# Attention, soft-MoE routing and FFN on one core: the routing's steps placed by a table in place of a queue

## Chip, cores and metric

One core of a Trainium2 chip runs the whole program in one launch. The metric is the device time of an execution in microseconds, the median of several runs.

## What is computed

Three layers follow each other: masked attention with ALiBi-like biases (4 batches, 8 heads, 768 tokens, head size 64, each token sees its last 96 keys and 8 global ones), a soft mixture of experts (32 slots, 8 experts), and a feed-forward layer with a squared ReLU.

```python
scores = scale * np.matmul(q, k.transpose(0, 1, 3, 2)) + bias     # masked to local and global keys
a = np.exp(scores - scores.max(-1)); a = a / (a.sum(-1) + 1e-09)
x = (a @ v) as (3072, 512)
logits = x @ phi                                                  # (3072, 32)
d = softmax(logits, axis=0); slot_input = d.T @ x                 # over all tokens
slot_out[e] = np.maximum(slot_input[e] @ w1[e], 0.0) @ w2[e]
c = softmax(logits, axis=1); y = c @ slot_out
out = np.maximum(y @ w_in, 0.0) ** 2 @ w_out
```

## The kernel before

The attention is cut into 48 units: a batch, a pair of query tiles of 128 tokens, and a pair of heads. Four units make a chunk of 256 tokens with all heads; there are 12 chunks. One pass of the loop at line 548 (`for i in range(2, NU - 4, 2)`) handles two units, so a chunk takes two passes. What TensorE does in a pass is the same each time, in this order: `stage_T` (line 265) turns the two units' weights `sm` with 16 transposes of 128x128 into four PSUM tiles `pt`; `stage_qk` (225) makes the scores `s` of a unit four ahead; `stage_pv` (281) multiplies the copied `pT` by the values into `o`, for both units; a second `stage_qk` makes another `s`. In the first chunk of a batch's three, some tiles have one key tile in place of two, so 12 transposes and narrower scores. Around it VectorE masks the scores and finds their maxima (`stage_max`, line 237, eight instructions a pass) and copies the first `pt` tile of each unit to `pT`; ScalarE takes the exponentials (`stage_exp`, 256), copies the second `pt` tile of each unit, and copies `o` to `xT` (`stage_x`, 299).

PSUM has eight banks here: four take the scores (tag `s`), four everything else (tag `m`, `bank` in line 305): the four `pt` tiles of a pass, the two `o`, and what the routing needs.

The routing is the generator `route` (323). For each finished chunk k it makes the logits and adds the chunk to the running softmax over tokens. Its `yield`s cut it into steps. For an odd k (a "front") there are six: the logits' matmuls `lt` (16 rows in the profile, line 362), their copies by ScalarE and VectorE, four transposes `pl` (372), then VectorE's `rc`, `lh`, and the reduction into `c_tok` with the first four transposes `px` of the chunk's output (341), then VectorE's multiply of `px` into `xb` (344) and the other four `px`, and the last multiply. An even k ("back") goes on after that for two chunks at once: a transpose `pq` of `c_tok` (413), a maximum and two exponentials (428 to 433), a transpose `pd` (445), its copy `db` and `rden`, a matmul `pS` of 4 x 512 columns (470), and the update of `acc` (488): eleven steps.

Which step runs where is set by `queue` and `step` (493 to 501). A chunk's route is appended when the chunk is done (line 550); `step(n)` lets the oldest route in the queue go n steps on. A pass calls it after the scores (`step(1)`, 567), after the second exponentials (`step(1)`, 572) and at its end (`step(2)`, 590); in the first pass of a chunk also right behind the units' transposes (554). Each engine runs its instructions in the program's order, so a step that is called elsewhere stands elsewhere on TensorE, VectorE and ScalarE. Which bank a tile gets is chosen when the program is built, by which one comes free first in that order.

After the loop (`K, L = LAST, LAST + 1`) the last two chunks' routing is written out by hand, then come the experts' layers and the feed-forward layer, whose weights SP loads as buffers come free.

Of the kernel before, what the change touches and what calls it, by code (L numbers as in the profile page):

```python
# [21 lines left out]
NPR = H // 2  # L22
# [17 lines left out]
def attention_moe_ffn(ctx: ExitStack, tc, qk, vx, nn, phi, w1, w2, w_in, w_out, consts, relw, out):  # L40
# [60 lines left out]
    def load_qk(i):  # L101
        b, tp, pr = units[i]
        r = early.pop("raw", None) if i == 0 else raw_tile(i)
        n = 5 if tp == 0 else 6
        nc.sync.dma_start(r[:, 0:n], qk[b, tp, pr][:, 0:n])
        raws[i] = r

    def load_v(i):
        b, tp, pr = units[i]
        v = early.pop("v", None) if i == 0 else v_tile(i)  # L110
        n = 3 if tp == 0 else 4
        nc.sync.dma_start(v[:, 0:n], vx[b, tp, pr][:, 0:n])
        vals[i] = v
# [58 lines left out]
    def make_flag():  # L172
        V.tensor_scalar(fl[:, 0:1], n_f[0:1, 0:1], 1.0, None, op0=ALU.is_lt)
        V.scalar_tensor_tensor(fl[:, 0:1], n_f[0:1, 0:1], float(LMAX), fl[:, 0:1], op0=ALU.is_gt, op1=ALU.add)
        V.scalar_tensor_tensor(fl[:, 0:1], n_f[0:1, 1:2], 0.0, fl[:, 0:1], op0=ALU.not_equal, op1=ALU.add)
        V.scalar_tensor_tensor(fl[:, 0:1], n_f[0:1, 2:3], 0.0, fl[:, 0:1], op0=ALU.is_lt, op1=ALU.add)
        V.scalar_tensor_tensor(fl[:, 0:1], n_f[0:1, 2:3], float(GMAX), fl[:, 0:1], op0=ALU.is_gt, op1=ALU.add)
        V.scalar_tensor_tensor(fl[:, 0:1], n_f[0:1, 3:4], 0.0, fl[:, 0:1], op0=ALU.not_equal, op1=ALU.add)
        V.tensor_copy(gen_i, fl[:, 0:1])
# [19 lines left out]
    def load_w(i, part=0, parts=1):  # L199
        name, src, shape, dt = items[i]  # L200
        if name == first[0][0]:

            t = slot(SLOTS[i], [P, 2, shape[1]], dt, "raw_0")
            for j in range(2):
                wt[first[j][0]] = t[:, j, :]
        elif SLOTS[i] == "s0":
            wt[name] = [slot(f"s0{h}", [P, 4, DM], dt, f"{name}{h}") for h in "ab"]
            for h in range(2):
                nc.sync.dma_start(wt[name][h], src[:, 4 * h : 4 * h + 4])
            return  # L210
        elif part == 0 and name != first[1][0]:
            wt[name] = slot(SLOTS[i], shape, dt, name)
        n = shape[1] // parts
        ps = slice(part * n, part * n + n)
        nc.sync.dma_start(wt[name][:, ps], src[:, ps])
# [9 lines left out]
    def stage_qk(i):  # L225
        b, tp, pr = units[i]
        r = raws.pop(i)
        sc = [aps.tile([P, 2, 2, P], F32, tag="s", name=f"s{i}_{hh}", bufs=4) for hh in range(2)]
        for tt in range(2):
            n = width(tp, tt)  # L230
            for hh in range(2):
                r0 = hh * D
                rhs = r[r0 : r0 + D, 2 + tt : 3 + tt, :] if n == 1 else r[r0 : r0 + D, 2 + tt : 6 - tt : 3 - 2 * tt, :]
                nc.tensor.matmul(sc[hh][:, tt, 0:n, :], lhsT=r[r0 : r0 + D, tt, :], rhs=rhs, start=True, stop=True)  # L234
        st[i] = [sc]

    def stage_max(i, tt):
        b, tp, pr = units[i]
        if tt == 0:
            st[i].append(att.tile([P, 4, 2, P], F32, tag="sm", name=f"sm{i}", bufs=3))  # L240
            st[i].append(att.tile([P, 4], F32, tag="nm", name=f"nm{i}", bufs=3))
        sc, sm, nm = st[i]
        n = width(tp, tt)
        for hh in range(2):
            j = 2 * tt + hh
            m = masks[2 * pr + hh]
            V.tensor_tensor_reduce(  # L247
                out=sm[:, j, 0:n, :], in0=sc[hh][:, tt, 0:n, :], in1=m[:, 2:3, :] if n == 1 else m[:, 0:2, :], scale=-QK_SCALE,
                scalar=3.0e38, op0=ALU.add, op1=ALU.min, accum_out=nm[:, j : j + 1])
# [6 lines left out]
    def stage_exp(i, tt):  # L256
        b, tp, pr = units[i]
        sm, nm = st[i][1], st[i][2]
        n = width(tp, tt)
        for hh in range(2):  # L260
            j = 2 * tt + hh
            nc.scalar.activation(sm[:, j, 0:n, :], sm[:, j, 0:n, :], AF.Exp, bias=nm[:, j : j + 1], scale=-1.0,  # L262
                                 accum_out=chunk_sums(i // NPR)[:, tt, 2 * pr + hh : 2 * pr + hh + 1])

    def stage_T(i):
        b, tp, pr = units[i]
        sm = st[i][1]
        pp = []
        for tt in range(2):
            pp.append(aps.tile([P, 2, 2, P], F32, tag="s" if i >= NU - 2 else "m", name=f"pt{i}_{tt}", bufs=4))  # L270
            for hh in range(2):
                for c in range(width(tp, tt)):
                    nc.tensor.transpose(pp[tt][:, hh, c, :], sm[:, 2 * tt + hh, c, :], ident)  # L273
        st[i] = pp, early.pop("pT") if i == 0 else pT_tile(i)

    def stage_ev(i, tt, eng):
        pp, pT = st[i]
        n = width(units[i][1], tt)
        eng(pT[:, 2 * tt : 2 * tt + 2, 0:n, :], pp[tt][:, :, 0:n, :])  # L279

    def stage_pv(i):
        b, tp, pr = units[i]
        v = vals.pop(i)
        pT = st[i][1]
        o = aps.tile([P, 2, P], F32, tag="s" if i == NU - 1 else "m", name=f"o{i}", bufs=4)
        for tt in range(2):
            n = width(tp, tt)
            for c in range(n):
                for hh in range(2):
                    nc.tensor.matmul(o[hh * D : hh * D + D, tt, :], lhsT=v[:, c * 3 if tt == 0 else 1 + c, hh * D : hh * D + D],  # L290
                                     rhs=pT[:, 2 * tt + hh, c, :], start=c == 0, stop=c == n - 1)
        st[i] = o
# [6 lines left out]
    def stage_x(i):  # L299
        nc.scalar.copy(chunk_x(i // NPR)[:, units[i][2], :], st.pop(i).rearrange("p a c -> p (a c)"))  # L300
# [11 lines left out]
    def route_start():  # L312
        G.memset(acc, 0.0)
        G.memset(rden, 0.0)
        run["nm"] = post.tile([P, 1], F32, tag="nmr", name="nm0", bufs=2)
        G.memset(run["nm"], 3.0e38)
# [4 lines left out]
    LAST = NT // TB - 2  # L321
# [168 lines left out]
                run["top"] = post.tile([P, 1], F32, tag="top", name="top")  # L490
                V.tensor_copy(run["top"], pm[:, 0:1])

    queue = []

    def step(n):
        while n and queue:
            try:
                next(queue[0])
                n -= 1
            except StopIteration:  # L500
                queue.pop(0)

    stage_qk(0)
    stage_qk(1)
# [41 lines left out]
    load_v(5)  # L546

    for i in range(2, NU - 4, 2):
        if i % NPR == 0:
            queue.append(route(i // NPR - 1, False, (i // NPR - 1) % 2 == 0))  # L550
        stage_T(i)
        stage_T(i + 1)
        if i % NPR == 0:
            step(1)
        stage_ev(i, 0, V.tensor_copy)
        stage_max(i + 3, 0)
        stage_exp(i + 2, 0)
        stage_ev(i, 1, nc.scalar.copy)
        stage_ev(i + 1, 0, V.tensor_copy)
        stage_exp(i + 2, 1)  # L560
        stage_ev(i + 1, 1, nc.scalar.copy)
        stage_max(i + 3, 1)
        stage_qk(i + 4)
        stage_exp(i + 3, 0)
        if i == 2:
            route_start()
        step(1)
        stage_pv(i)
        stage_pv(i + 1)
        stage_x(i)  # L570
        stage_exp(i + 3, 1)
        step(1)
        stage_max(i + 4, 0)
        stage_qk(i + 5)
        stage_max(i + 4, 1)
        stage_x(i + 1)
        for j in (i + 7, i + 8):
            if 9 <= j < NU:
                load_qk(j)
        for j in (i + 4, i + 5):  # L580
            if j < NU:
                load_v(j)
        for j in (i - 4, i - 3):
            if 0 <= j < NPRE * PARTS:
                load_w(j // PARTS, j % PARTS, PARTS)
        if i == 8:
            make_flag()
        if i == 12:
            cond = nc.values_load(gen_i, min_val=0, max_val=8)
        step(2)  # L590
    step(1)
    assert not queue


    K, L = LAST, LAST + 1
    i = NU - 4
# [164 lines left out]
    with tc.block(name="last"):  # L761
# [25 lines left out]
        z = slotZ.rearrange("p (e r) -> p e r", r=ZS)[:, :, 0 : 4 * NS].rearrange("p e (k s) -> p e k s", s=NS)  # L787
# [53 lines left out]
    with tc.If(cond != 0, label="dense"):  # L841
# [3 lines left out]
        a = ta.rearrange("p a c -> p (a c)").rearrange("p (a c) -> p a c", c=F)  # L845
# [261 lines left out]
    for c0 in range(0, WIDTHS[0], P):  # L1107
        c = slice(c0, c0 + P)
# [207 lines left out]
```

## Time and profile before

| | us |
|---|---|
| median of 3 runs | 518.91 |
| lowest, highest | 518.76, 520.04 |
| the profiled execution, its own time | 518.86 |
| its span, first to last instruction | 517.1 |
| TensorE busy | 509.3 |
| VectorE busy | 378.1 |
| ScalarE busy | 310.5 |
| GpSimd busy | 151.8 |

The span is 1.8 us shorter than the execution's time, which holds what lies before the first and after the last instruction. The loop that the change touches runs from 19.2 us to 162.1 us of the span. "Busy" of TensorE holds its pipeline's modelled ends, so how long a group of its instructions takes is read from the start of that group to the start of the next.

### The profile page before, as it was taken

Reading aid. Unit: us, or ns where it says so; the run is one execution under the profiler, and the core shown is the slowest. Engines: PE = TensorE matmul, PEld = TensorE weight load, DVE = VectorE, ACT = ScalarE, POOL = GpSimd, SP = SyncE. Lnnn points to the kernel's source line nnn. Section 1 sums busy time; section 2 is a strip of 40 time slices with the busy share of each in tenths; the row PEclk is TensorE's granted clock in tenths of the full one; section 3 lists DMA queues with packets and bytes.
Section 4 is the critical chain, followed back from the end, with each engine's and each line's share of the span. In section 5 each row is a group of like instructions: output and inputs, shape, how many; then the busy total and the mean of one; then the engine's idle time right before and its main releaser. Section 6 shows DMA issues by size and latency. Waiting matters only on the chain.

```text
span 517.1 us, 10074 instructions
## 1 busy us (share of the span) xinstructions
PE 509.3 (98%) x3626; PEld 392.4 (76%) x3626; DVE 378.1 (73%) x937; ACT 310.5 (60%) x828; POOL 151.8 (29%) x137
## 2 busy tenths in 40 slices
PE   9999999999999999999999999999999999999997
PEld 6777777677777734578787888878888788888886
DVE  7788978887878746697598987967748667445553
ACT  6978878787788203397964655446535445434440
POOL 7000000000000110001344775447644437534441
PEclk9999999999999999999999999999999999999999
DMA  8889999999894899913404040210300000003233
GB/s 273 275 281 306 364 300 321 326 333 301 307 337 140 281 385 421 380 36 129 162 1 162 1 163 2 71 52 0 124 0 1 0 2 1 1 20 121 106 121 122
DMA packets 25976, 86.95 MB, mean 168 GB/s; under 512 B 2882, under 2 KB 5442, under 8 KB 23746
## 3 DMA queue, kind: packets, MB, share of 16 engines
q1 hardware_dynamic: 25776, 86.13, 46.5%
q8 instruction: 30, 0.49, 0.4%
q14 instruction: 24, 0.20, 0.1%
q10 hardware_dynamic: 146, 0.13, 0.1%
HBM read 79.95 MB, written 6.29 MB: 167 GB/s over the span
## 4 chain that ended last, share of the span: by engine, by line
PE 55%; DVE 3%; ACT 2%; POOL 1%; issue 1%; POOLq 0%; DVEq 0%
PE acc L1040 15%; PE acc L1041 15%; PE acc L1042 15%; PE h L1016 4%; PE pSO L922 3%; POOL g L1026 1%; DVE rg L1023 1%; ACT rg L1022 1%; PE pre L818 1%; DVE oacc L1049 0%; PE pu L982 0%; PE pc L883 0%; PE pu L990 0%; DVE cvyi L932 0%; PE pu L1110 0%
## 5 line engine op out<-in xcount | busy, mean ns | idle before, releaser
L1026 POOL TENSOR_TENSOR g<-rg,g 128x512 fp32r<-128x512 f32 x96 | 117.6, 1228 | 121.2 <-DVE rg L1023 118.5
L1040 PE MATMUL acc<-w,g 128*128 128x512 f32 (+1 forms) x387 | 152.0, 393 | 0.4 <-ACT oacc_p L1047 0.4
L1041 PE MATMUL acc<-w,g 128*128 128x512 f32 (+1 forms) x387 | 151.2, 391 | 0.0
L1042 PE MATMUL acc<-w,g 128*128 128x512 f32 (+1 forms) x387 | 150.1, 388 | 0.0
L1022 ACT ACTIVATE rg<-h 128x512 f32<-128x512 f32 (+1 forms) x109 | 59.7, 548 | 115.9 <-PE h L1016 107.8
L262 ACT ACTIVATE sm<-sm,nm 128x256 f32<-128x256 f32 (+1 forms) x192 | 92.7, 487 | 1.0 <-DVE nm L247 0.9
L1040 PEld LDWEIGHTS acc<-w,g 128*128 128x128 f32 x387 | 72.7, 188 | 16.9 <-ACT rg L1022 1.5
L1042 PEld LDWEIGHTS acc<-w,g 128*128 128x128 f32 x387 | 72.7, 188 | 16.2 <-DVE g L1026 0.5
L1023 DVE SCALAR_TENSOR_TENSOR rg<-h,rg 128x512 f32<-128x512 f32 (+1 forms) x109 | 67.9, 623 | 21.5 <-ACT rg L1022 21.4
L1041 PEld LDWEIGHTS acc<-w,g 128*128 128x128 f32 x387 | 73.0, 189 | 10.9
L1049 DVE TENSOR_TENSOR oacc_p<-acc,oacc_p 128x512 f32<-128x512 f32 x63 | 43.4, 688 | 45.0 <-PE acc L1042 44.9
L247 DVE CUSTOM_DVE_ANT_0 sm<-s,mask 128x256 f32<-128x256 f32 (+1 forms) x192 | 66.9, 397 | 2.5 <-ACT sm L262 1.2
L1025 ACT ACTIVATE g<-rg 128x512 fp32r<-128x512 f32 (+1 forms) x109 | 63.4, 581 | 3.5
L234 PE MATMUL s<-raw 64*128 64x256 f32 (+1 forms) x384 | 52.3, 393 | 0.1
L672 POOL TENSOR_TENSOR lh<-lh 128x256 f32<-128x256 f32 x1 | 0.7, 728 | 157.8 <-PE pt L273 157.8
L273 PE MATMUL pt<-con,sm 128*128 128x128 f32 x352 | 45.4, 276 | 1.6 <-ACT pT L279 1.6
L290 PE MATMUL o<-pT,v 128*64 128x128 f32 x704 | 44.3, 276 | 0.0
L273 PEld LDWEIGHTS pt<-con,sm 128*128 128x128 f32 x352 | 38.5, 141 | 7.0 <-ACT pT L279 2.8
L290 PEld LDWEIGHTS o<-pT,v 128*64 128x64 f32 x704 | 37.9, 137 | 7.0 <-ACT sm L262 2.1
L234 PEld LDWEIGHTS s<-raw 64*128 64x128 f32 x384 | 31.9, 192 | 14.7 <-DMA v<-in_vx 6.5
L1016 PEld LDWEIGHTS h<-cu 128*128 128x128 f32 x192 | 36.0, 188 | 7.7 <-DVE cu L1112 0.2
L1016 PE MATMUL h<-cu 128*128 128x256 f32 x192 | 40.4, 281 | 0.0
(220 smaller groups left out, 564.3 us busy)
## 6 DMA issues: line engine op xcount, KB each, us to landing
w<-in_w SPq DMA_DIRECT2D x40, 512.0 KB, 6.6
raw<-in_qk SPq DMA_DIRECT2D x32, 384.0 KB, 6.0
w<-in_w SPq DMA_DIRECT2D x5, 2048.0 KB, 9.1
v<-in_vx SPq DMA_DIRECT2D x32, 256.0 KB, 4.0
raw<-in_qk SPq DMA_DIRECT2D x16, 320.0 KB, 4.9
win<-in_w_in SPq DMA_DIRECT2D x2, 2048.0 KB, 8.8
wout<-in_w_out SPq DMA_DIRECT2D x2, 2048.0 KB, 7.9
out_x<-oacc_p SPq DMA_DIRECT2D x15, 256.0 KB, 2.0
```

What stands on the lines that cost most here:

```text
L234: nc.tensor.matmul(sc[hh][:, tt, 0:n, :], lhsT=r[r0 : r0 + D, tt, :], rhs=rhs, start=True, stop=True)
L247: V.tensor_tensor_reduce(out=sm[:, j, 0:n, :], in0=sc[hh][:, tt, 0:n, :], in1=m[:, 2:3, :] if n == 1 else m[:, 0:2, :], scale=-QK_SCALE, s ...
L262: nc.scalar.activation(sm[:, j, 0:n, :], sm[:, j, 0:n, :], AF.Exp, bias=nm[:, j : j + 1], scale=-1.0, accum_out=chunk_sums(i // NPR)[:, tt ...
L273: nc.tensor.transpose(pp[tt][:, hh, c, :], sm[:, 2 * tt + hh, c, :], ident)
L290: nc.tensor.matmul(o[hh * D : hh * D + D, tt, :], lhsT=v[:, c * 3 if tt == 0 else 1 + c, hh * D : hh * D + D], rhs=pT[:, 2 * tt + hh, c, : ...
L1016: nc.tensor.matmul(ph[:, k, :], lhsT=U[:, c0 : c0 + P], rhs=cst[:, n * TB : n * TB + TB], start=True, stop=True)
L1022: nc.scalar.activation(r, ph[:, k0:k1, :], AF.Relu)
L1023: V.scalar_tensor_tensor(g, ph[:, k0:k1, :], 0.0, r, op0=ALU.max, op1=ALU.mult)
L1026: (G if q else V).tensor_tensor(g2[:, 1, js, :], g, g2[:, 0, js, :].bitcast(F32), op=ALU.subtract)
L1040: nc.tensor.matmul(pa[:, cs], lhsT=ghi[:, j, ms], rhs=whi[:, j, cs], start=j == 0, stop=False)
L1041: nc.tensor.matmul(pa[:, cs], lhsT=ghi[:, j, ms], rhs=wlo[:, j, cs], start=False, stop=False)
L1042: nc.tensor.matmul(pa[:, cs], lhsT=glo[:, j, ms], rhs=whi[:, j, cs], start=False, stop=j == J - 1)
```

## The change

The queue goes. A table gives for each route a list of places: how many units behind the chunk's end (`di`, in steps of two units, one pass) and which of four call sites of the pass (`a` behind the units' transposes, now in every pass; `b` and `c` where they were; `z` at the end). Odd chunks use FRONT, even ones BACK; the last two routes of the loop (k = 8 and 9) have lists of their own in NEAR.

```diff
-    queue = []
-    def step(n):
-        while n and queue:
-            try:
-                next(queue[0])
-                n -= 1
-            except StopIteration:
-                queue.pop(0)
+    FRONT = ((0, "b"), (0, "c"), (0, "z"), (2, "z"), (4, "b"), (4, "z"))
+    BACK = ((0, "b"), (0, "c"), (0, "z"), (2, "z"), (4, "a"), (4, "z"), (6, "a"), (6, "z"), (8, "a"), (8, "a"), (8, "b"))
+    NEAR = {
+        LAST - 2: BACK[:6] + ((6, "a"), (6, "b"), (6, "c"), (6, "z"), (6, "z")),
+        LAST - 1: FRONT[:3] + ((2, "a"), (2, "c"), (2, "z")),
+    }
+    plan = {}
+    for k in range(LAST):
+        for di, at in NEAR.get(k, FRONT if k % 2 else BACK):
+            plan.setdefault((k * NPR + NPR + di, at), []).append(k)
+    routes = {}
+    def step(i, at):
+        for k in plan.pop((i, at), ()):
+            if k not in routes:
+                routes[k] = route(k, False, k % 2 == 0)
+            next(routes[k], None)
...
     for i in range(2, NU - 4, 2):
-        if i % NPR == 0:
-            queue.append(route(i // NPR - 1, False, (i // NPR - 1) % 2 == 0))
         stage_T(i)
         stage_T(i + 1)
-        if i % NPR == 0:
-            step(1)
+        step(i, "a")
...
-        step(1)
+        step(i, "b")
...
-        step(1)
+        step(i, "c")
...
-        step(2)
-    step(1)
-    assert not queue
+        step(i, "z")
+    assert not plan
```

No instruction is added or taken away on any engine; rows only change places. Three places follow.

TensorE, the end of the pass with units 16 and 17 and the start of the next, where chunk 3's `pl` stands. The words in brackets name the engine that a row waits for (here mostly for its PSUM bank). Before:

```order
L372 MATMUL pl_1179<-con,lt_1152 128x128 [waits DVE_49,Activation_49]
L372 MATMUL pl_1179<-con,lt_1152 128x128 x3
L341 MATMUL px_0_1190<-con,xT_906 128x128 [waits PE_49]
L341 MATMUL px_0_1190<-con,xT_906 128x128 x3
L273 MATMUL pt_0_1195<-con,sm_1040 128x128 x4
L273 MATMUL pt_1_1200<-con,sm_1040 128x128 [waits Activation_49]
L273 MATMUL pt_1_1200<-con,sm_1040 128x128 x3
L273 MATMUL pt_0_1206<-con,sm_1096 128x128 [waits DVE_49,PE_49]
L273 MATMUL pt_0_1206<-con,sm_1096 128x128 x3
L273 MATMUL pt_1_1211<-con,sm_1096 128x128 [waits Activation_49]
L273 MATMUL pt_1_1211<-con,sm_1096 128x128 x3
```

With the change:

```order
L413 MATMUL pq_1157<-con,c_tok 128x128 [waits Activation_49]
L372 MATMUL pl_1159<-con,lt_1129 128x128 [waits Activation_49]
L372 MATMUL pl_1159<-con,lt_1129 128x128 x3
L273 MATMUL pt_0_1164<-con,sm_1011 128x128 [waits DVE_49]
L273 MATMUL pt_0_1164<-con,sm_1011 128x128 x3
L273 MATMUL pt_1_1169<-con,sm_1011 128x128 [waits Activation_49]
L273 MATMUL pt_1_1169<-con,sm_1011 128x128 x3
L273 MATMUL pt_0_1175<-con,sm_1074 128x128 [waits Activation_49]
L273 MATMUL pt_0_1175<-con,sm_1074 128x128 x3
L273 MATMUL pt_1_1180<-con,sm_1074 128x128 [waits DVE_49]
L273 MATMUL pt_1_1180<-con,sm_1074 128x128 x3
```

The first `px` has moved a pass on, `pq` has come from between the scores and `o` to the front of the transposes, and the fourth `pt` tile of the pass waits for VectorE's copy of the first one, where it waited for ScalarE's copy of the second.

VectorE, from chunk 3's reciprocals to the first copy of `pt` behind them, before:

```order
L376 TENSOR_SCALAR rc_1118<-sums_768 128x16
L377 RECIPROCAL rc_1118<-rc_1118 128x16
L395 TENSOR_TENSOR lh_1186<-pl_1179,rc_1118 128x256 x2
L351 TENSOR_REDUCE c_tok<-lh_1186 128x64
L279 COPY pT_1205<-pt_0_1195 128x512
```

With the change:

```order
L376 TENSOR_SCALAR rc_1095<-sums_748 128x16
L377 RECIPROCAL rc_1095<-rc_1095 128x16
L395 TENSOR_TENSOR lh_1266<-pl_1159,rc_1095 128x256 x2
L351 TENSOR_REDUCE c_tok<-lh_1266 128x64
L453 COPY db_1297<-pd_1262 128x128
L462 SCALAR_TENSOR_TENSOR rden<-rden,fo_1188,dn_1189 128x1
L279 COPY pT_1285<-pt_0_1275 128x512
```

The block now reads a `pl` that was made a whole pass earlier, and stands one pass later, ahead of unit 20's copy in place of unit 18's; the back route's `db` and `rden` stand behind it.

VectorE at the start of the loop's last pass (units 42 and 43), before:

```order
L376 TENSOR_SCALAR rc_2454<-sums_2118 128x16
L377 RECIPROCAL rc_2454<-rc_2454 128x16
L395 TENSOR_TENSOR lh_2517<-pl_2510,rc_2454 128x256 x2
L351 TENSOR_REDUCE c_tok<-lh_2517 128x64
L279 COPY pT_2536<-pt_0_2526 128x512
```

With the change:

```order
L428 TENSOR_REDUCE rmax_2518<-pq_2488 128x1
L429 SCALAR_TENSOR_TENSOR nm_1_2517<-rmax_2518,nm_1_2082 128x1
L376 TENSOR_SCALAR rc_2431<-sums_2096 128x16
L377 RECIPROCAL rc_2431<-rc_2431 128x16
L395 TENSOR_TENSOR lh_2528<-pl_2490,rc_2431 128x256 x2
L351 TENSOR_REDUCE c_tok<-lh_2528 128x64
L279 COPY pT_2505<-pt_0_2495 128x512
```

Chunk 8's maximum has come in ahead of chunk 9's block, and both stand ahead of the first copy of the pass.

## Rows read from the trace of the kernel before

**Rows 1.** The page's busy time of each engine, share of the span, instructions

```profile
PE 509.3 (98%) x3626; PEld 392.4 (76%) x3626; DVE 378.1 (73%) x937; ACT 310.5 (60%) x828; POOL 151.8 (29%) x137
```

**Rows 2.** Busy time by stretch: loop, and experts' layers; last clock, DMA share, GB/s

```profile
19.17:162.12 142.95, 141.11 (x1537) 106.21 (x1535) 119.84 (x473) 115.67 (x429) 0.00 (x0) 1.00 0.88 300
...
182.01:220.13 38.12, 37.94 (x337) 17.67 (x338) 21.99 (x41) 10.78 (x23) 2.52 (x4) 1.00 0.96 391
```

**Rows 3.** Timeline of TensorE: start, length, instruction, count, idle before and releaser

```profile
69.22 0.60 PE L341 MATMUL px<-con,xT 128*128 128x128 f32 x4
69.66 1.47 PE L273 MATMUL pt<-con,sm 128*128 128x128 f32 x12
71.43 0.66 PE L273 MATMUL pt<-con,sm 128*128 128x128 f32 x4 [0.29 <-ACT pT L279]
72.01 1.14 PE L234 MATMUL s<-raw 64*128 64x256 f32 x8
73.08 0.66 PE L341 MATMUL px<-con,xT 128*128 128x128 f32 x4
73.67 1.97 PE L290 MATMUL o<-pT,v 128*64 128x128 f32 x32
75.56 1.13 PE L234 MATMUL s<-raw 64*128 64x256 f32 x8
76.63 1.97 PE L273 MATMUL pt<-con,sm 128*128 128x128 f32 x16
78.52 0.66 PE L362 MATMUL lt<-xT,phib 64*32 64x256 f32 x16
```

**Rows 4.** Waits in the loop: who for whom, us in total, times, longest

```profile
PE pt L273 <- ACT pT L279: 1.6, 5, 0.4
...
DVE lh L395 <- PE pl L372: 6.8, 9, 1.5
```

**Rows 5.** Timeline of all engines where a fourth `pt` tile waits

```profile
126.69 0.76 DVE L395 TENSOR_TENSOR lh<-pl,rc 128x256 f32<-128x256 f32 x2 [1.48 <-PE pl L372]
...
126.87 1.47 PE L273 MATMUL pt<-con,sm 128*128 128x128 f32 x12
127.48 1.05 DVE L351 TENSOR_REDUCE c_tok<-lh 128x64 f32<-128x512 f32 x1
127.99 0.58 ACT L279 COPY pT<-pt 128x512 f32<-128x512 f32 x1 [1.06 <-PE pt L273]
128.44 0.68 DVE L279 COPY pT<-pt 128x512 f32<-128x512 f32 x1
```

**Rows 6.** Timeline of TensorE where `lt`, and transposes behind eight `px`, take longer

```profile
84.24 2.14 PE L273 MATMUL pt<-con,sm 128*128 128x128 f32 x16
86.31 0.93 PE L234 MATMUL s<-raw 64*128 64x128 f32 x8
...
134.87 1.08 PE L362 MATMUL lt<-xT,phib 64*32 64x256 f32 x16
135.89 1.13 PE L234 MATMUL s<-raw 64*128 64x256 f32 x8
```

**Rows 7.** Timeline of VectorE: `db`, copies, maxima, reciprocals

```profile
61.48 0.29 DVE L453 COPY db<-pd 128x128 f32<-128x128 f32 x1 [0.94 <-PE pd L445]
...
61.91 0.69 DVE L279 COPY pT<-pt 128x512 f32<-128x512 f32 x1
62.52 0.41 DVE L247 CUSTOM_DVE_ANT_0 sm<-s,mask 128x256 f32<-128x256 f32 x1
...
62.86 0.42 DVE L247 CUSTOM_DVE_ANT_0 sm<-s,mask 128x256 f32<-128x256 f32 x1
...
67.66 0.17 DVE L376 TENSOR_SCALAR rc<-sums 128x16 f32<-128x16 f32 x1
67.86 0.25 DVE L377 RECIPROCAL rc<-rc 128x16 f32<-128x16 f32 x1
```

**Rows 8.** Timeline of ScalarE: one exponential

```profile
156.76 0.51 ACT L262 ACTIVATE sm<-sm,nm 128x256 f32<-128x256 f32 x1
```

**Rows 9.** Waits of SP's queue from 150 us to 225 us

```profile
SPq L209 <- PE o L290: 4.3, 1, 4.3
```

## The prediction

> **What bounds the kernel now.** I read the page's engine table first: TensorE is busy in 509.3 of 517.1 us, the next engine, VectorE, in 378.1 [rows 1]. Then the busy time by stretch: in the loop TensorE is busy in 141.11 of 142.95 us, and its granted clock stands at 1.00 of full speed, the level of 2.4 GHz [rows 2]. So the loop ends when TensorE has gone through its list, and only two things can shorten it: a group of its instructions that takes less, or a wait that goes. The third view is TensorE's own timeline, read from the start of a group to the start of the next, because the lengths printed hold pipeline ends. Sixteen `pt` transposes in front of a matmul take 78.52 − 76.63 = 1.89 us; a scores group 1.07 (76.63 − 75.56); the two `o` 1.89 (75.56 − 73.67) [rows 3]. The same view gives the price of changing kind: four `px` in front of `pt` take 69.66 − 69.22 = 0.44, four `px` in front of `o` 73.67 − 73.08 = 0.59 [rows 3]. Transposes run on into transposes; a transposing group that a matmul follows pays **0.15 us** more.
>
> The fourth view, the waits, shows what TensorE itself waits for: five times a fourth `pt` tile for ScalarE's copy of the second one, 1.6 us idle in all, 0.4 at most; and VectorE's `lh` nine times for `pl`, 6.8 us [rows 4]. The fifth view, all engines about such a place, shows why. `pl` and `px` have taken banks, so four `pt` tiles must do with three: the fourth begins at 128.63, behind ScalarE's copy (127.99 + 0.58 = 128.57) [rows 5]. From the first `pt` to the next scores that is 129.22 − 126.87 = 2.35 us where an undisturbed pass takes 1.89, so **0.46 us** a time [rows 3, 5].
>
> **The change part by part.**
>
> *Transposing groups.* No instruction is added on any engine; in the built program's order I count 37 transposing groups on TensorE inside the loop before and 28 after. Before, 15 stood alone between matmuls (five `pl`, five `pq`, five `px`); after, six do (the five second `px` of the odd chunks, and chunk 8's `pd`). The other places now join `pt`: `pl` and the back chunks' first `px` at the end of a pass, their second `px` right behind `pt`, `pq` and `pd` at the end of a pass. Nine exits at 0.15 [rows 3]: **−1.35 us**. All lie on TensorE, so all count.
>
> *Waits of before that go.* The five fourth tiles: 1.6 us idle [rows 4] and 0.17 each for the extra exit and start (0.46 − 0.29), 2.5 in all, the same as five times 0.46 with one of 0.68. `lt` directly behind `pt`: once 135.89 − 134.87 = 1.02, undisturbed 0.59, so 0.43 [rows 6], and 0.15 another time. `pt` behind eight `px`: 86.31 − 84.24 = 2.07 over 1.89 is 0.18 in the first such place [rows 6], five of them 0.6. Some 20 smaller excesses of 0.05 to 0.15 about `pd`, `px` and `pl`: 1.45. Together 5.1 us: **−5.1** if nothing took their place.
>
> *Waits that come.* `pl` is now made at the end of one pass and read at the end of the next, and the first `px` is made at the end of one pass and read, in an odd chunk, behind the scores of the next. In 19 of the loop's 20 passes behind the first some tile therefore holds a bank across the four `pt`, and the fourth waits for the first's reader, in most passes VectorE's copy. No row shows this wait; I build it from rows. Four tiles of four transposes take 0.44 each [rows 3], so the fourth is due 1.31 us after the first starts. A copy starts 1.12 us after a group whose second tile it reads (126.87 to 127.99) [rows 5], which is 0.25 after that tile's end, so the first tile's copy may start at 0.44 + 0.25 = 0.69. It lasts 0.69 [rows 7], and the release takes 0.06 (128.57 to 128.63) [rows 5]: 1.44, so **0.13 us late if VectorE is free**. Is it? Its work in a pass is two copies at 0.61 and eight maxima at 0.34, start to start [rows 7], 3.94, so it is done about 4.66 us into the pass. Where rc (0.45) [rows 7], `lh` (0.79) and the reduction (0.96) [rows 5] come behind, it is done at 6.86, and with `db` and `rden` (0.43) [rows 7] at 7.29. TensorE's pass ahead of that is 1.89 + 1.07 + 1.89 + 1.07, four `px` at 0.44 and a `pd` at 0.11, 6.47; the copy could start at 6.47 + 0.69 = 7.16. So where a front's block and a back's `db` both precede the copies (passes 12, 20, 28, 36), VectorE is 0.13 late: 0.13 + 0.13, taken as 0.28. That gives:
>
> - four such passes at 0.28: 1.1
> - nine passes where VectorE is free, at 0.13: 1.2
> - five passes where the holder is a `px` that VectorE multiplies away, between 0 and 0.3, taken at 0.15: 0.75
> - the last pass (42 and 43), where chunk 8's maximum and chunk 9's block stand ahead of the first copy, and `dT` and `fo`, two exponentials of up to 0.51 [rows 8], stand on ScalarE ahead of its copy: two more waits, estimated at 0.95
> - some ten places where a `pl`, `px` or `pd` stands a little sooner behind its input than it could, at 0.05 [rows 3, 6]: 0.5
>
> Sum **+4.5 us**, 0.23 a pass. Its ends: 0 if VectorE is always early enough, and, if every pass pays what the five pay now, 20 × 0.46 plus 0.5 more in the last pass = 9.7. I take the middle value because the releaser changes from ScalarE's second copy to VectorE's first, which can start 0.43 sooner. The Trainium skill, page "PSUM — Partial Sum Buffer", section "Summary: rules for kernel authors", says to evacuate PSUM promptly, since it is tight; the table does the contrary with `pl` and the first `px`, and by that rule every pass would pay the 0.46 that the row shows, and the sum would be a loss.
>
> *Other queues.* VectorE's 6.8 us for `pl` [rows 4] mostly go, since `pl` is a pass old when it is read; that is worth nothing by itself, as VectorE ends no pass. It matters only as the slack that makes its copies early. ScalarE gets nothing new but the order, except in the last pass, counted above. SP's and POOL's rows inside the loop keep their order. GpSimd has nothing in the loop [rows 2].
>
> *After the loop.* Between 182 and 220 us the DMA engines are 0.96 busy, at 391 GB/s [rows 2]. SP issues the weights' loads as buffers come free, which the attention's last `o` releases (4.3 us of waiting) [rows 9], so the loads come forward with the loop, and I take nothing off the gain.
>
> **Sum:** −1.35 − 5.1 + 4.5 = −1.95 us. The profiled execution's own time is 518.86, 1.8 over its span and 0.05 under the median of the runs shown, so **516.9 us**. Bounds: 518.86 − 6.45 = 512.4 without any new wait, 518.86 − 6.45 + 9.7 = 522.1 with all.
>
> **The rivals.**
>
> 1. *Faster: VectorE is nearly always early.* Losing 6.8 us of waiting for `pl` [rows 4] could bring VectorE ahead everywhere. Then only the 0.13 at ten places and the 0.5 stay, 1.8: 518.86 − 6.45 + 1.8 = **514.2**. For it speaks that VectorE idles long before `lh` (1.48 us at 126.69 [rows 5]); against it that these waits stood behind its maxima, so that its block begins late in the pass anyway. Chance 0.20.
> 2. *No change: the weights' loads set the end.* With the DMA share at 0.96 [rows 2], the gain could be lost behind the loop and the time be **518.9**. Against it: TensorE is 37.94 of 38.12 us busy in that stretch [rows 2], and SP waits for TensorE, not the reverse [rows 9]. A smaller kin of it, that the new waits eat the gain exactly, is counted here too. Chance 0.13.
> 3. *Slower: held banks cost more than the exits.* `pl` and `px` keep a bank through every pass, where before only five passes lost 0.46 [rows 5]. If each of the 20 loses 0.46, the new waits are 9.2 and the time is 518.86 − 6.45 + 9.2 = **521.6**. It decides from 6.45 / 20 = 0.32 us a pass; I have 0.23. For it: VectorE's margin in the passes with a block is below zero by the working above. Against it: the 0.46 came from ScalarE's copy of the second tile, and the first tile is copied sooner. Chance 0.12.
>
> That the change does not do what it says is excluded by the order: the rows move as the table states.
>
> **How the numbers follow.** The forecast, 0.55, has its own range from 515.7 to 518.1: the uncertainty of the new waits is about a quarter of 4.5 to each side. No change, for this kernel, means within 0.3%, 1.56 us, about what a measurement can tell: 517.35 to 520.47. Two thirds of the forecast's part (0.37) and rival 1 (0.20) lie below it: faster 0.57. The other third (0.18) and rival 2 (0.13) make the same 0.31, rival 3 slower 0.12. The range goes from 513.9, a little under rival 1, to 519.2, a little above rival 2; outside are rival 3 and some 0.08 below.
>
> **What the changed profile would show.** Right: the loop ends near 160.1 us in place of 162.12; `pl` and `pd` are followed by `pt` with no step; the waits of `pt` for ScalarE's copy go and waits of `pt` for VectorE's copy come, in most passes, of 0.1 to 0.3; `lh` no longer waits for `pl`; the pass with units 42 and 43 is about 1 us longer in its transposes. Wrong: fourth `pt` tiles of 0.4 or more over their due time in most passes (rival 3); no idle at `pt` at all (rival 1); the loop 2 us shorter, but TensorE waiting for a DMA or a semaphore of SP's loads later (rival 2).

## The result and the profile after

| | before | changed |
|---|---|---|
| median, us | 519.15 (7 runs) | 522.73 (7 runs) |
| lowest, highest | 518.76, 520.04 | 521.10, 523.38 |
| profiled execution, its time and span | 518.86, 517.1 | 523.22, 521.4 |

The ratio is 1.0058, 95% interval 1.004 to 1.0076: the change makes the kernel **slower**, by 3.6 us between the medians, where 516.9 was forecast; that is 0.58%, past the 0.3% that the prediction took for no change. The seven runs fall into two groups, and their mean granted clock tells them apart: four runs at 0.996 took 522.73 to 523.38, three at 0.999 to 1.000 took 521.10 to 521.56. The profiled run is one of the first kind.

The page's engine table of the changed kernel, beside [rows 1], shows TensorE 3.3 us busier with the same instructions:

```profile
PE 512.6 (98%) x3626; PEld 392.7 (75%) x3626; DVE 379.0 (73%) x937; ACT 310.7 (60%) x828; POOL 151.8 (29%) x137
```

The busy time by stretch tells where. The columns are those of [rows 2]; the stretches are the loop from unit 4 on (as in [rows 2]), the four `pt` tiles of the pass behind the loop (units 44 and 45), and the 3.41 us in which the granted clock (the third number from the end) stands low:

```profile
19.59:162.14 142.55, 141.44 (x1537) 105.65 (x1535) 117.56 (x462) 115.35 (x428) 0.00 (x0) 1.00 0.88 303
162.14:167.01 4.87, 3.06 (x21) 1.97 (x17) 4.77 (x17) 2.54 (x9) 0.00 (x0) 0.84 0.63 215
165.50:168.91 3.41, 3.17 (x30) 1.81 (x30) 2.61 (x9) 1.70 (x5) 0.00 (x0) 0.50 0.03 12
```

The loop is a little shorter, 142.55 in place of 142.95 us. The four `pt` tiles of the pass behind it take 4.87 us, of which TensorE is busy in 3.06; the kernel before does them in 1.89 (164.01 − 162.12), back to back:

```profile
162.12 1.97 PE L273 MATMUL pt<-con,sm 128*128 128x128 f32 x16
164.01 1.06 PE L639 MATMUL lt<-xT,phib 64*32 64x256 f32 x16
```

TensorE's timeline of the changed kernel at that place, and the start of what follows:

```profile
162.14 0.66 PE L273 MATMUL pt<-con,sm 128*128 128x128 f32 x4
162.99 0.66 PE L273 MATMUL pt<-con,sm 128*128 128x128 f32 x4 [0.19 <-DVE xb L344]
165.02 0.70 PE L273 MATMUL pt<-con,sm 128*128 128x128 f32 x4 [1.38 <-DVE acc L488]
165.96 1.11 PE L273 MATMUL pt<-con,sm 128*128 128x128 f32 x4 [0.24 <-ACT pT L279]
167.01 1.11 PE L644 MATMUL lt<-xT,phib 64*32 64x256 f32 x16
168.04 2.37 PE L290 MATMUL o<-pT,v 128*64 128x128 f32 x32
170.34 1.09 PE L273 MATMUL pt<-con,sm 128*128 128x128 f32 x8
```

From the first `pt` to unit 46's `pt` it takes 170.34 − 162.14 = 8.20 us, before 166.90 − 162.12 = 4.78. That is 3.4 of the 4.3 us between the two spans (521.4 − 517.1). The rest: the loop begins 0.42 later and is 0.40 shorter, and from unit 46's `pt` to the end it takes 351.1 us in place of 350.2, and most of that difference is weights that land late ("Loads behind the loop" below). The third tile waits 1.38 us for VectorE's `acc`, and the granted clock then falls: it is 0.50 from 165.50 to 168.91, the lower level of 1.2 GHz, and the `o` group takes 2.30 us in place of 1.90. At the full clock the same stop costs less: the run e4 below meets it too, and there this pass, at a clock of 1.00, takes 7.11 us, 2.3 more than before.

Why is `acc` late? All engines' timeline, VectorE's and ScalarE's lines and one of TensorE's:

```profile
158.54 0.21 DVE L462 SCALAR_TENSOR_TENSOR rden<-rden,fo,dn 128x1 f32<-128x1 f32 x1
...
161.14 1.06 PE L470 MATMUL pS<-xb,db 128*32 128x512 f32 x8
...
162.24 0.69 DVE L344 TENSOR_TENSOR xb<-px,rc 128x512 f32<-128x512 f32 x1 [3.49 <-PE pS L470]
...
163.36 0.51 ACT L262 ACTIVATE sm<-sm,nm 128x256 f32<-128x256 f32 x1 [3.01 <-DVE nm L247]
...
164.22 0.74 DVE L488 SCALAR_TENSOR_TENSOR acc<-acc,fo,pS 128x512 f32<-128x512 f32 x1
```

In the loop's last pass (units 42 and 43) VectorE stands still for 3.49 us in front of chunk 9's first multiply into `xb`. It does not wait for `px`, which it reads, but for `pS` of chunk 8. The odd chunks' `xb` is one buffer (line 328, `bufs=1`), and chunk 7's values lie in it until chunk 8's `pS`, which works on two chunks, has read them. The table places the multiply at (2, "c") for chunk 9, ahead of the scores' maxima, and that `pS` at (6, "z") for chunk 8, at the end of the same pass. Behind the multiply four maxima, `acc` and the copies of `pt` queue on VectorE, and behind the maxima ScalarE's exponentials (3.01 us of waiting). In the kernel before, chunk 8's `pS` ran in the pass of units 40 and 41.

What the forecast said of VectorE's waits came true beside it. These are VectorE's waits from 150 to 167 us, after; [rows 4]'s wait of `lh` for `pl` is not among them, nor among those of the whole loop:

```profile
DVE xb L344 <- PE pS L470: 3.5, 1, 3.5
DVE rmax L428 <- PE pq L413: 0.8, 1, 0.8
DVE lt L366 <- PE lt L362: 0.5, 1, 0.5
```

And this is a place in the loop where a first `px` keeps its bank across the four `pt` (units 40 and 41):

```profile
145.19 1.47 PE L273 MATMUL pt<-con,sm 128*128 128x128 f32 x12
146.85 0.66 PE L273 MATMUL pt<-con,sm 128*128 128x128 f32 x4 [0.18 <-DVE xb L344]
147.45 0.66 PE L341 MATMUL px<-con,xT 128*128 128x128 f32 x4
```

From the first `pt` to the `px` behind them it takes 147.45 − 145.19 = 2.26 us, against 1.74 (1.89 less the 0.15 of an exit) where nothing holds a bank and transposes follow: 0.52 of waiting.

### The profile page after: what moved, and what is told of

It reads as the page before. It is cut to its first block, busy times and chain, and to the rows that moved or that the text cites. A ratio compares the mean times of both kernels' runs of the same rounds, so it can differ in the third digit from the quotient of the medians.

```text
span 521.4 us, 10107 instructions
## 1 busy us (share of the span) xinstructions
PE 512.6 (98%) x3626; PEld 392.7 (75%) x3626; DVE 379.0 (73%) x937; ACT 310.7 (60%) x828; POOL 151.8 (29%) x137
## 4 chain that ended last, share of the span: by engine, by line
PE 57%; DVE 3%; ACT 2%; POOL 1%; issue 0%; DVEq 0%; POOLq 0%; ACTq 0%
PE acc L1045 16%; PE acc L1046 16%; PE acc L1047 15%; PE h L1021 4%; PE pSO L927 3%; DVE rg L1028 1%; PE pre L823 1%; POOL g L1031 1%; ACT rg L1027 1%; PE pu L987 0%; PE pc L888 0%; PE pu L995 0%; DVE oacc L1054 0%; PE pu L1115 0%; DVE cvyi L938 0%
## 5 line engine op out<-in xcount | busy, mean ns | idle before, releaser
L273 PE MATMUL pt<-con,sm 128*128 128x128 f32 x352 | 47.9, 279 | 2.6 <-DVE acc L488 1.4
```

## The experiments

Two questions were open: whether the loss is made by the last pass's stop or by held banks all through the loop, and where the loop's expected 2 us went. The table gives each run's median with its ratio to the kernel before and, from its profile, the length of the loop (from unit 4's first `pt` to unit 44's) and of the pass behind it (from there to unit 46's).

| | median us | ratio (95%) | loop | pass behind |
|---|---|---|---|---|
| before | 519.15 | | 142.95 | 4.78 |
| changed | 522.73 | 1.0058 (1.0040 to 1.0076) | 142.55 | 8.20 |
| e1 | 527.57 | 1.0167 (1.0153 to 1.0181) | 142.49 | 4.82 |
| e2 | 519.84 | 1.0011 (1.0002 to 1.0020) | 142.44 | 5.12 |
| e3 | 520.56 | 1.0033 (1.0018 to 1.0049) | 142.48 | 4.78 |
| e4 | 523.11 | 1.0068 (1.0054 to 1.0082) | 143.02 | 7.11 |
| e5 | 518.62 | 0.9986 (0.9977 to 0.9995) | 141.10 | 5.13 |
| e6 | 519.32 | 1.0002 (0.9993 to 1.0011) | 142.97 | 4.78 |
| e7 | 518.17 | 0.9980 (0.9971 to 0.9989) | 141.09 | 5.11 |
| e8 | 521.18 | 1.0036 (1.0022 to 1.0050) | 144.82 | 4.54 |
| e9 | 517.45 | 0.9957 (0.9942 to 0.9972) | 139.67 | 5.12 |
| e10 | 517.11 | 0.9950 (0.9934 to 0.9966) | 139.65 | 5.12 |

The kernel before, run beside them, had medians of 519.25 (e1 to e4), 519.13 (e5 to e8) and 519.40 (e9, e10). Where the loop begins differs between profiles, from 18.97 to 19.93 us, also between two whose program up to there is the same (before 19.17, e6 18.99), so loops are compared by length.

**e1: a buffer of its own for chunk 9's `xb`.** It takes the place of two `raw` tiles, which are free by then.

```diff
-        xb = post.tile(...) if back else att.tile([P, 2, DM], F32, tag="xb", name=f"xb{k}", bufs=1)
+        if apart and k == LAST - 1 and banks[0] is aps:
+            xb = Halves([att.tile([P, 6, P], F32, tag="raw", name=f"xb{k}_{t}", bufs=4)[:, 0:4, :].rearrange("p a b -> p (a b)") for t in range(2)])
+        else:
+            xb = post.tile(...) if back else att.tile([P, 2, DM], F32, tag="xb", name=f"xb{k}", bufs=1)
```

> The changed kernel, but chunk 9's xb gets memory of its own instead of the one buffer that chunk 7's xb still holds until chunk 8's pS has read it. Theory (the loss is VectorE standing still 3.49 us at that xb in the last pass, so that the pass behind the loop takes 8.2 us in place of 4.8 and the clock falls there): the wait for pS goes, the pass behind the loop comes near 5 us, the granted clock stays 1.00 and the time falls by 3 to 4.5 us, to 518.4 to 519.4. Rival (held banks cost in every pass of the loop): the loop stays as it is and so does the time, 521 to 523.

The stop is gone: no wait of `xb` for `pS`, 4.82 us behind the loop, the clock at 1.00 there. So the one buffer causes the stop. The time, expected at 518.4 to 519.4, is 527.57 all the same, for a reason of its own, so this run shows the cause of the stop and not its price. SP's waits from 150 to 240 us show it; the `raw` memory belongs to a weight's buffer after the attention, and SP may not load it until the last reader of `xb` is done:

```profile
SPq L209 <- PE pS L750: 18.2, 1, 18.2
```

Before, SP's longest wait at this line was 4.3 us for `o` [rows 9]. TensorE then waits for the weights at `pSO` (its timeline from 204 us):

```profile
204.96 3.64 PE L937 MATMUL pSO<-w,hZ 128*32 128x512 f32 x32
211.46 2.76 PE L937 MATMUL pSO<-w,hZ 128*32 128x512 f32 x16 [2.87 <-DMA w<-in_w]
216.39 6.14 PE L937 MATMUL pSO<-w,hZ 128*32 128x512 f32 x32 [2.17 <-DMA w<-in_w]
```

**e2: the same stop taken away by order alone.**

```diff
-        LAST - 1: FRONT[:3] + ((2, "a"), (2, "c"), (2, "z")),
+        LAST - 1: FRONT[:3] + ((2, "a"), (2, "z"), (2, "z")),
```

> The changed kernel, but chunk 9's second-last step (the first multiply into xb, the second px) is placed at the end of the last pass, behind chunk 8's pS and acc, in place of ahead of its scores. Theory (VectorE standing still ahead of its maxima): the maxima and copies no longer wait behind xb, VectorE's wait is under 1.5 us, the pass behind the loop is shorter by 1 to 3 us and the time is 518.8 to 521. Rival (held banks in the loop): 521 to 523, since the loop's other passes are untouched.

One place in one list moves the median by 2.9 us, from 522.73 to 519.84, with the loop as long as it was (142.44). VectorE's waits from 150 to 167 us are now

```profile
DVE acc L488 <- PE pS L470: 1.6, 1, 1.6
DVE rmax L428 <- PE pq L413: 0.8, 1, 0.8
```

and the 1.6 lies behind the maxima, which no longer wait. The time is in the theory's range and outside the rival's. The theory's other two figures are just missed: the wait is 1.6 us, not under 1.5, and the pass behind is 3.08 us shorter (8.20 − 5.12), not 1 to 3.

**e3: the places of before for chunks 8 and 9 only.**

```diff
+    BACK0 = ((0, "a"), (0, "b"), (0, "c"), (0, "z"), (0, "z"), (2, "b"), (2, "c"), (2, "z"), (2, "z"), (4, "a"), (4, "b"))
+    FRONT0 = ((0, "b"), (0, "c"), (0, "z"), (0, "z"), (2, "b"), (2, "c"))
-    NEAR = {
...
-    }
+    NEAR = {LAST - 2: BACK0, LAST - 1: FRONT0}
```

> The changed kernel with the places of before for the last two routes of the loop (chunks 8 and 9); chunks 0 to 7 keep FRONT and BACK. Theory (the loss is made by the lists of chunks 8 and 9): no stop behind the loop, the pass there 4.8 us, the time 518 to 519. Rival (FRONT and BACK cost in the loop): 520.5 to 522.5.

The pass behind the loop is 4.78 again, as expected, and the loop 142.48, but the time misses the theory's range by 1.6 us: 520.56. That number lies at the edge of the rival's range, but not by the rival's mechanism, since the loop is 0.47 us shorter than before's. The loss lies behind the attention. From unit 46's `pt` to the end this profile has 519.4 − 167.02 = 352.4 us, before 517.1 − 166.90 = 350.2. TensorE waits there for weights (its timeline from 204 us):

```profile
205.58 8.25 PE L926 MATMUL pSO<-w,hZ 128*32 128x512 f32 x72
214.05 1.05 PE L926 MATMUL pSO<-w,hZ 128*32 128x512 f32 x4 [0.22 <-DMA w<-in_w]
215.32 1.05 PE L926 MATMUL pSO<-w,hZ 128*32 128x512 f32 x4 [0.21 <-DMA w<-in_w]
216.30 0.88 PE L887 MATMUL pre<-con,cr 128*128 128x128 f32 x6
```

These 80 matmuls and the two breaks take 216.30 − 205.58 = 10.72 us, before 8.77. That raised the question of e6 and e7.

**e4: the places of before for chunks 0 to 7, the change's lists for 8 and 9.**

```diff
+    NEAR.update({k: FRONT0 if k % 2 else BACK0 for k in range(LAST - 2)})
```

> The places of before for chunks 0 to 7, and the change's own lists for chunks 8 and 9 alone. Theory: the stop behind the loop comes with these lists, so the time is as that of the whole change, 521 to 523.5, and VectorE waits over 3 us for pS in the last pass. Rival (the loop's other passes make the loss): 518.5 to 519.5.

523.11: these two lists alone make the whole loss. VectorE waits 3.4 us for `pS` again. The clock fell in this profile too, but 18 us behind the stop, from 185.14 to 188.55 us, in `pre`.

**e5: e2, with `pl` behind the four `pt` in place of ahead of them** (all but chunk 9's).

```diff
-    FRONT = ((0, "b"), (0, "c"), (0, "z"), (2, "z"), ...
-    BACK = ((0, "b"), (0, "c"), (0, "z"), (2, "z"), ...
+    FRONT = ((0, "b"), (0, "c"), (2, "a"), (2, "z"), ...
+    BACK = ((0, "b"), (0, "c"), (2, "a"), (2, "z"), ...
-        LAST - 1: FRONT[:3] + ((2, "a"), (2, "z"), (2, "z")),
+        LAST - 1: ((0, "b"), (0, "c"), (0, "z"), (2, "a"), (2, "z"), (2, "z")),
```

> The changed kernel with chunk 9's last steps behind chunk 8's pS (as in the run that moved them), and with every pl but chunk 9's right behind the four pt in place of ahead of them, so that it still joins transposes but holds no bank across pt. Theory (a bank held across pt costs 0.1 to 0.25 us a pass): the ten or so passes with pl lose their excess, the loop is 1.2 to 1.6 us shorter than with pl ahead (141 us in place of 142.4). Rival (the fourth pt waits for VectorE being late, whoever holds banks): loop within 0.4 us of 142.4. For the time: 518.0 to 518.8 if the loop's gain reaches the end; 519.3 to 520.3 if the weights' loads behind the loop set the end.

The loop falls by 1.34 us, from 142.44 to 141.10 (expected were 1.2 to 1.6), with the same number of changes of kind: a held `pl` does cost. The time, 518.62, is in the range for a gain that reaches the end, 518.0 to 518.8.

**e6 and e7: before and e5, each without one weight load.** Expert 7 takes expert 6's second matrix; 2 MB less to load.

```diff
         name, src, shape, dt = items[i]
+        if name == "w2_7":
+            wt[name] = wt["w2_6"]
+            return
```

> The kernel before without the last expert's second weight load (2 MB; expert 7 uses expert 6's matrix), so that the loads behind the loop end about 5 us sooner. If the loads do not bind it, the time stays within 0.5 us of 519.2; if they bind it, it falls by 1 us or more.

> The kernel with pl behind pt, again without the last expert's second weight load. Theory (the loop's gain is lost to the loads behind it): against the kernel before with the same load left out it is faster by as much as its loop is shorter, 1.5 to 2.2 us, and its pSO group takes 8.7 us without a wait. Rival (the loss behind the loop is something else): no faster than that kernel by more than 0.7 us.

Before does not gain (519.32): its loads do not bind it. Without the load e5 is 1.15 us faster than before (518.17 against 519.32), with it 0.51 (518.62 against 519.13). The 0.45 us between e5 and e7 is within the noise of the medians (their intervals overlap); their profiles show it clearly, the 80 `pSO` matmuls taking 9.49 us with the load and 8.72 without. So a part of the gain is held back by the loads behind the loop. The 1.15 is under the theory's 1.5 to 2.2 and over the rival's 0.7; e5's loop is 1.85 us shorter than before's, but the pass behind it 0.35 longer.

**e8: every transposing group of the routing behind `pt`**, `pq` with the second `px`, VectorE's block behind the copies (a new call place "d").

```diff
+    FRONT = ((0, "b"), (0, "c"), (2, "a"), (2, "d"), (2, "z"), (4, "a"), (4, "z"))
+    BACK = ((0, "b"), (0, "c"), (2, "a"), (2, "d"), (2, "z"), (4, "a"), (4, "z"), (6, "a"), (6, "d"), (6, "c"), (6, "z"))
+    NEAR = {LAST - 1: FRONT[:5] + ((2, "z"), (2, "z"))}
...
                 turn(t, range(NPR))
+                if t and back and apart:
+                    pq = bank(f"pq{k}")
+                    nc.tensor.transpose(pq..., c_tok..., ident)
                 yield
                 rows(t)
+                if not t and apart and banks[0] is aps:
+                    yield
...
```

> A table in which every transposing group of the routing (pl, both px, pq, pd) stands right behind the four pt, and what VectorE does for it stands behind the pass's copies and maxima, so that no bank but the chunk 9's is held across pt. Theory (held banks make the new waits): waits at pt fall from 4.7 us to under 2.5, the loop from 142.5 to 139.5 to 141, the time 517 to 519.5. Rival (VectorE's lateness makes them): its blocks now push the copies late, waits at pt as before or more, loop 142 or over, time 519.5 to 522.

The waits at `pt` are gone, as the theory said, and the loop, 144.82 us, is longer, as the rival said: neither had the mechanism. TensorE's waits in the loop:

```profile
PE o L290 <- DVE lt L366: 2.9, 5, 0.6
PE o L290 <- ACT xT L300: 2.4, 5, 0.5
PE px L341 <- DVE pT L279: 0.6, 2, 0.3
```

`px`, `pq` and two `lt` now stand behind `pt` at once and fill the four banks; the first `o` of a pass waits for `lt`'s copies and the second for the copy of the first, five times each. The same shortage came up at another place.

**e9: e5, with only the even chunks' first `px`, and chunk 9's, right behind `pl`**, and its multiply into `xb` at the end of that pass.

```diff
-    BACK = ((0, "b"), (0, "c"), (2, "a"), (2, "z"), (4, "a"), (4, "z"), ...
+    BACK = ((0, "b"), (0, "c"), (2, "a"), (2, "d"), (2, "z"), (4, "a"), (4, "z"), ...
-        LAST - 2: BACK[:6] + ((6, "a"), (6, "b"), (6, "c"), (6, "z"), (6, "z")),
-        LAST - 1: ((0, "b"), (0, "c"), (0, "z"), (2, "a"), (2, "z"), (2, "z")),
+        LAST - 2: BACK[:7] + ((6, "a"), (6, "b"), (6, "c"), (6, "z"), (6, "z")),
+        LAST - 1: ((0, "b"), (0, "c"), (2, "a"), (2, "d"), (2, "z"), (2, "z")),
...
                 rows(t)
+                if not t and back and apart and banks[0] is aps:
+                    yield
...
         stage_max(i + 3, 1)
+        step(i, "d")
         stage_qk(i + 4)
```

> The kernel with pl behind pt, and now also the even chunks' first px right behind pl and its multiply at the end of the same pass (so only their second px is left behind the next pt), and chunk 9's pl and first px in the same way. Theory (held banks make the waits at pt): the excess of 0.5, 0.35 and 0.5 us in the passes where such a px was held, and that of the last pass, goes; the loop is 139 to 140 us where it was 141.1. Time 517.0 to 518.0 where half of it is lost to the loads behind the loop, 518.6 if all is. Rival (VectorE's block of 2.2 us behind the copies makes the next copies late): loop 141 to 142, time 518.6 to 519.6.

The loop is 139.67 us, 1.43 less than e5's, and 517.45 us is **better than both kernels** (ratio to before 0.9957, interval 0.9942 to 0.9972); both are in the theory's ranges. The pass of units 40 and 41, above 2.26 us in the changed kernel, now reads (TensorE's timeline)

```profile
143.19 1.97 PE L273 MATMUL pt<-con,sm 128*128 128x128 f32 x16
145.01 0.66 PE L341 MATMUL px<-con,xT 128*128 128x128 f32 x4
...
150.38 1.91 PE L273 MATMUL pt<-con,sm 128*128 128x128 f32 x16
152.12 0.60 PE L372 MATMUL pl<-con,lt 128*128 128x128 f32 x4
153.24 0.66 PE L341 MATMUL px<-con,xT 128*128 128x128 f32 x4 [0.52 <-ACT pT L279]
```

145.01 − 143.19 = 1.82 us, and in the loop's last two passes one wait is left, where chunk 9's `px` comes too early.

**e10: e9 without the same weight load.**

> The same kernel without the last expert's second weight load (2 MB; expert 7 uses expert 6's matrix). Theory (the loads behind the loop keep part of the gain): 0.4 to 1.3 us faster than with the load. Rival (the loads never bind): the same within 0.3 us.

517.11 against 517.45: 0.34 us, between the two expectations, and the two intervals overlap. The profiles show the waiting more clearly than the medians: the 80 `pSO` matmuls take 212.88 − 203.05 = 9.83 us with the load (to the next group),

```profile
203.05 9.90 PE L930 MATMUL pSO<-w,hZ 128*32 128x512 f32 x80
212.88 0.87 PE L891 MATMUL pre<-con,cr 128*128 128x128 f32 x6
```

and 211.95 − 203.23 = 8.72 us without it:

```profile
203.23 8.79 PE L933 MATMUL pSO<-w,hZ 128*32 128x512 f32 x80
211.95 0.87 PE L894 MATMUL pre<-con,cr 128*128 128x128 f32 x6
```

## Why the prediction was wrong

**Transposing groups: right.** I compared each group in the loop with the shortest length of its kind in front of the same kind of neighbour. These least lengths sum to 137.28 us before and 136.02 after, −1.26 where −1.35 was forecast. The sums depend on what counts as the same kind: other sortings give −0.7 to −1.5, so this part and the next two are known to about half a microsecond.

**Waits that go: right in size.** The excess over the least lengths was 5.67 us before; the sum had 5.1. The largest of its terms, 0.46 a time, rests on these two rows of TensorE before, which follow those of [rows 5]:

```profile
128.63 0.66 PE L273 MATMUL pt<-con,sm 128*128 128x128 f32 x4 [0.29 <-ACT pT L279]
129.22 0.93 PE L234 MATMUL s<-raw 64*128 64x128 f32 x8
```

**Waits that come: under-sized.** In the loop they are 6.53 us, not 4.5. By terms: the four passes where a front's block and `db` precede the copies, 1.23 (forecast 1.1); the nine with VectorE free, 1.30 (1.2); the last pass, 0.69 (0.95); these three hold. The five passes where VectorE multiplies a held `px` away cost 0.08, 0.51, 0.35, 0.06 and 0.52, 1.52 together where 0.75 was taken, with 0.3 as the end of each: the multiply itself (0.69 in the rows above) stands on VectorE ahead of the copies. The small excesses at `pl`, `px`, `pq`, `pd`, `s` and one `o` are 1.8, not 0.5. So the loop gives −0.40, not −1.95; a mechanism that was right with two terms of the sum too small.

**The last pass: the step that failed.** The prediction gave it two waits, 0.95 us, and ended its account at the loop's end; it took "chunk 8's maximum and chunk 9's block" as all that stood ahead of VectorE's copies. It missed that chunk 9's multiply, the next step of the same list, writes the one `xb` that chunk 8's `pS` had still to read. No row of before shows that wait, because there the `pS` came a pass earlier; the buffer's count in line 328 and the order of the two steps would have shown it. Its price in the profile is 3.4 us, the pass behind the loop, the clock's fall included, and 2.3 at the full clock (e4). With a term missing, even the upper bound of 522.1, "with all" new waits, lies below the measured 522.73. e1 and e2 show the cause by taking it away in two ways (e1 in the profile only, e2 in the time too), e4 shows it alone.

**The clock.** It was taken as 1.00 throughout. In the profiled run it falls right behind the stop. Of the other runs only the mean is known: 522.73 to 523.38 us where it is 0.996, 521.10 to 521.56 where it is not, so some 1.9 us more. Of the other kernels only e4, with the same stop, and e1, with its waits for weights, have runs with a mean below 0.999.

**Loads behind the loop: half wrong.** That the loads come forward with the loop holds for when SP issues them: the last six begin 14.4 us ahead of the 80 `pSO` matmuls that need them, before and in the changed kernel (205.23 − 190.86, 208.77 − 194.29), and in e9 too. It does not hold for when they land, and so "I take nothing off the gain" does not. Before, with the last of the six (issued at 197.12) and its time to landing in us:

```profile
190.86 6.70 SPq L215 DMA_DIRECT2D w<-in_w  x6
w<-in_w SPq DMA_DIRECT2D x1, 512.0 KB, 15.8
205.23 8.84 PE L922 MATMUL pSO<-w,hZ 128*32 128x512 f32 x80
214.00 0.87 PE L883 MATMUL pre<-con,cr 128*128 128x128 f32 x6
```

With the change (the last issued at 199.54):

```profile
194.29 6.67 SPq L215 DMA_DIRECT2D w<-in_w  x6
w<-in_w SPq DMA_DIRECT2D x1, 512.0 KB, 17.8
208.77 9.61 PE L927 MATMUL pSO<-w,hZ 128*32 128x512 f32 x80
218.32 0.88 PE L888 MATMUL pre<-con,cr 128*128 128x128 f32 x6
```

Before, the last load lands at 212.97 us, 0.43 ahead of the matmuls that read it (213.40). With the change it lands at 217.29 and those matmuls begin at 217.34, and the group takes 9.55 us in place of 8.77. The same holds in e2, e3, e5, e8 and e9: their last matmuls begin 0.04 to 0.05 us after the landing, and the group takes 9.36 (e8) to 10.72 us (e3). The loss does not follow the loop's length: e8 has the longest loop and e9 the shortest (9.83). From the first of the six issues to the last landing it takes 22.1 us before and 22.0 in e4, the two with the old places for chunks 0 to 7, and 22.9 to 24.3 in the other kernels with all loads, e1 apart. The share of DMA in that stretch was shown [rows 2]; the waits of SP for TensorE [rows 9] only say when a load starts, not when it lands.

**The rivals.** The sign is that of the third, but not its mechanism: held banks cost 0.24 us a pass at `pt` (4.7 over 20), under its point of 0.32, and e2 without the stop is 1.0011 of before. The mechanism of the second, late weights, is there too, with 0.78 us. As for the Trainium skill's rule, page "PSUM — Partial Sum Buffer", section "Summary: rules for kernel authors", to evacuate promptly: e5 and e9 agree with its direction, −1.34 and −1.43 us of loop for reading tiles in the pass that makes them. The 0.46 in every pass that the prediction worked out by it did not come, and e8, which reads still more tiles early, has a loop 2.38 us longer than e2's.

What stays open: why the loads take longer to land with the new places (e3's last lands 2.3 us later than before's though the six are first issued within 0.2 us of the same time), why the clock falls in some runs of one program and not in others, and how much of the 1.8 us of small excesses is VectorE's and how much ScalarE's.

## What to carry to other kernels

When a step is moved, list the buffers that it writes as well as those it reads, with their counts, and ask which reader of the old contents it now runs ahead of: on an engine that works in order, everything behind that write waits as well. Treat the first and last rounds of a pipelined loop as cases of their own, up to the first group that runs undisturbed again. And before counting a gain, look by how much the data for the next stage arrive ahead of their use: here the last weights had 0.43 us to spare, and up to 2 us (e3) went to waiting for them.

## What was not expected of the hardware

A stop of 1.38 us on TensorE was followed by 3.4 us at half clock, and by the mean clock not in every run of the same program; neither TensorE's earlier waits of up to 0.4 us in the loop [rows 4] nor those of 0.6 us in e8's loop, whose run has a mean clock of 1.0, did that. And a stage whose last load lands only 0.43 us ahead of its use gave no sign of it in the profile before: no wait for a DMA stood at `pSO`, and leaving 2 MB out gained nothing (519.32 against 519.13); yet with the new places the same loads, issued as far ahead, landed 0.7 to 2.2 us later behind their issue, and the group lost 0.6 to 2.0 us to them.
